# Second mixture-of-experts layer: token rows turned a step or two later for two tiles, check counts issued later, gathers issued one part per step

## The chip, the cores and the metric

The kernel runs on one core of a Trainium2 chip. The metric is the time of one execution on the device in microseconds (us). Before the change the median of three runs is 853.89 us (852.45 to 854.54).

Engines are named as the profile names them: PE is TensorE (its matmuls; PEld are its weight loads), DVE is VectorE, ACT is ScalarE, POOL is GpSimd, SP is SyncE. Each engine works through its own instructions in order. SBUF is the on-chip memory; PSUM is the small memory into which PE writes, in banks.

## The reference

Three layers follow each other. Only the last one is touched by the change.

```python
def reference(**kwargs):
    attn_out = _attn_ref(**attn_kwargs)                 # 4 x 8 heads, 768 positions, window 128 and 4 sink keys
    x = np.ascontiguousarray(attn_out.transpose(0, 2, 1, 3)).reshape(B * S, H * D)   # 3072 tokens x 512
    x = _moe_ref(x=x, **moe_kwargs)                     # 8 experts, the best one per token, scaled by its gate
    return _moe2_ref(x=x, **moe2_kwargs)

def _moe2_ref(x, w_gate, w1, w2):
    N, D = x.shape                                      # 3072, 512
    E = w_gate.shape[1]                                 # 8 experts
    cap = N // E                                        # each takes 384 tokens
    logits = x @ w_gate
    order = np.argsort(-logits.flatten())
    assigned, counts = -np.ones(N, int), np.zeros(E, int)
    for idx in order:                                   # best (token, expert) pairs first
        tok, e = idx // E, idx % E
        if assigned[tok] >= 0 or counts[e] >= cap:
            continue
        assigned[tok] = e; counts[e] += 1
    for e in range(E):
        mask = assigned == e
        out[mask] = np.maximum(x[mask] @ w1[e], 0) @ w2[e]
    return out
```

## The kernel before

The last layer (function `moe2`) handles eight **tiles**, numbered 0 to 7 here. A tile is one expert with its 384 tokens. Which expert fills up first, and with which tokens, is not known until the chip has worked it out, so the routing of tile k+1 runs on the side while PE multiplies tile k.

**The multiplication** (`Ffn.run`). A tile has 8 steps, one for each block of 128 hidden values. In step s PE makes 12 matmuls of the first layer (`ph`, line 1036), ACT and DVE split the result into two parts (`hh`, `hl`, lines 1046 and 1047), and PE makes 9 matmuls of the second layer for the block of two steps earlier (`y`, line 950). Every number is carried as a high and a low part, so three matmuls stand for one. The inner function `side(q)` is called at four places of a step, q = 0 to 3: after half of the first layer, after the rest of it, after the first three matmuls of the second layer, and at its end. There a weight block is split (ACT makes `w1h` and `w2h`, DVE or POOL makes `w1l` and `w2l`), the rows of the next tile are turned, and the routing goes a piece on (`tick`).

**Rows of the next tile.** POOL gathers the 384 token rows of a tile by three indirect DMAs of 128 rows (`xget`, line 1893), then copies the expert's number (`em3`), for which the load of the second half of the weights waits. The rows are **turned** in four parts, d = 0 to 3: three transpositions by PE into the PSUM bank `tr` (line 796), then ACT copies them out (`xh`, line 797) and DVE makes the rest (`xl`, line 798). The bank `tr` exists once, so a turn waits until ACT and DVE have emptied it of the turn before. The table `xp=((6, 0), (6, 2), (7, 0), (7, 2))` says where: part 0 in step 6 at q = 0, part 1 in step 6 at q = 2, and so on.

**The routing** (`Route.steps`, `compact_steps`). Tokens of an expert are found by a search for a threshold: DVE compares (`cmp`), PE counts (`rt<-OH,cmp`, line 1693), DVE reduces, PE spreads the result (line 1976), DVE sets the next bound, two to four times per tile. Then comes the **compaction**: sums on PE (line 1498), ranks on DVE (`r`), one-hot rows in two halves and their factors on DVE (`ohb`, `ft`), and a chain of 26 matmuls on PE (`rc<-ft,ohb`, line 1523), from which DVE reads the row numbers (`idx`). Two **check counts** stand beside it: the number of tokens taken (`rc<-A,ones`, line 1517, read by ACT at line 1902 into `ckj`) and the number of tokens by expert (`rc<-OH,ones`, lines 1967 and 2033, read by ACT into `ckm`). They are only compared with what they should be at the very end. All of these write to different columns of one PSUM tile, `rc`. POOL copies one number per search step (`hold`, line 1957), between its other work.

The order on each engine is the order in which the code issues it. The generators of the routing are advanced at every `tick`; they go on when a small model of the clock, kept while the program is built, says that PE and DVE are far enough.

Of the kernel before, what the change touches and what calls it, by code (L numbers as in the profile page):

```python
# [13 lines left out]
I32 = mybir.dt.int32  # L14
# [11 lines left out]
E, F = 8, 1024  # L26
# [753 lines left out]
class Ffn:  # L780
# [37 lines left out]
    def warm(self, k):  # L818
        p = self.ps.tile([128, 512], F32, name="y0")
        for _ in range(k):  # L820
            self.nc.tensor.matmul(p, self.g.wz[:, 0:128], self.g.wz, start=True, stop=True)

    def run(self, js, w1, w2, src, yout, hook=None, xp=((6, 0), (6, 2), (7, 0), (7, 2)), LEAD=3, LAG=2, pre=None, onx=None, more=(), mark=lambda s, n: None):


        nc, wk, ps, clk = self.nc, self.wk, self.ps, self.g.clk
# [47 lines left out]
        def poll_x():  # L874
            if wantx and (wantx[0] == js[0] or st[0] >= min(8 * alljs.index(wantx[0]) - XO, total - 8)) and src.ready_x(wantx[0]):
                j = wantx[0]
                if j not in asked:
                    src.xids(j)
                    asked[j] = src.wait
                if asked[j] == 0:  # L880
                    xgs[wantx.pop(0)] = src.xget(j)
                else:
                    asked[j] -= 1
# [48 lines left out]
        def prep(j, d, tag="tr"):  # L932
            if j not in xgs:
                src.force_x(j)
                clk.pe = max(clk.pe, clk.dve)
                wantx.remove(j)
                xgs[j] = src.xget(j)
            if d == 0 and onx is not None:
                onx(j, xgs[j])
            self.xprep(j, src.width(j), xgs[j], d, tag)  # L940

        def tick():
            if hook is not None:
                hook()
            poll_w(2)
            poll_x()

        def mm3(o, pairs, w, first, end):
            for i, (l, r) in enumerate(pairs):
# [41 lines left out]
        for s in range(last + 1):  # L991
            st[0] = s
            jx, f = divmod(s, 8)

            def side(q):
                while q == 3 and late:
                    split(*late.pop(0))
                ticked = q == 3 and not self.vsplit and s + LEAD < total and (s + LEAD) % 2 == 0 and not late
                if ticked:
                    tick()  # L1000
                if q == 1 and late:
                    late.append((s, 1))
                else:
                    split(s, q)
                if jx + 1 < len(js) and s < total:
                    for d in range(4):
                        if xp[d] == (f, q):
                            prep(js[jx + 1], d)
                if not ticked:
                    tick()  # L1010

            if s < total and small(s):
                q = f % 4
# [39 lines left out]
            if s in second:  # L1053
                c = second[s][0]
                j1, f1 = divmod(c, 8)
                A = src.width(js[j1])
# [4 lines left out]
                parts = [(hh, hl, w2h, w2l, f1)]  # L1061
# [37 lines left out]
class Src:  # L1099
# [13 lines left out]

    force_x = xids = force_e
    wait = 0

    def ereg2(self, j):
        return self.ereg(j)
# [348 lines left out]
JC, NIT, FEW, IDLE = 64, 4, 2, (3, 2, 1)  # L1467
# [9 lines left out]
WT = 3, 2, (3, 6), (1, 3), 6, 2, 3, 9, 2, 2  # L1477
# [4 lines left out]
def compact_steps(nc, g, p, pi, A, rs, pre, tag, check=None, warm=lambda k: None, tcol=None, lag=0.2, wt=0, first=None):  # L1482

    clk = g.clk
    V = Vec(nc, clk)
    iob, tcol = g.iob, tcol or g.tcol
    n = A.shape[1]
    H = half(n)
    nd = tcol.shape[2]
    k = nd // 2  # L1490
    bs, acc, cnt = pi[:, 0:1], pi[:, 32:32 + 3 * nd], pi[:, 64:64 + n]
    pj = p.tile([128, k, 4], F32, name=tag + "pj", bufs=1)
    r = p.tile([128, 4, n], F32, name=tag + "r", bufs=1) if first is None else first
    r0, g0, g1, g2 = (r[:, i] for i in range(4))
    rb = p.tile([128, n], BF, name=tag + "rb", bufs=1)
    oh = p.tile([128, 2, 128, H], BF, name=tag + "ohb", bufs=1)
    ft = p.tile([128, n, nd, 3], BF, name=tag + "ft", bufs=1)
    nc.tensor.matmul(bs, g.tri, rs, start=True, stop=True, skip_group_check=True)
    nc.scalar.activation(g0, A, AF.Copy)
    warm(wt)  # L1500
    yield 0.0
    V.scalar_tensor_tensor(r0, pre, bs, A, op0=OP.add, op1=OP.mult)
    V.tensor_scalar(g1, r0, 128.5, None, op0=OP.is_ge)
    V.tensor_scalar(g2, r0, 256.5, None, op0=OP.is_ge)
    V.scalar_tensor_tensor(r0, g1, -128.0, r0, op0=OP.mult, op1=OP.add)
    V.scalar_tensor_tensor(rb, g2, -128.0, r0, op0=OP.mult, op1=OP.add)
    yield 0.0
    cuts = [(0, 0, H)] + ([(1, 0, n - H)] if first is None else [(1, 0, 8), (1, 8, n - H)])
    for q, o, w in cuts:
        V.tensor_tensor(oh[:, q, :, o:w], iob[:, :, 0:w - o], bc(rb[:, None, H * q + o:H * q + w], [128, 128, w - o]), op=OP.is_equal)  # L1510
        if q == 0:
            V.tensor_tensor(ft, bc(r[:, 1:4, :, None].rearrange("p a n w -> p n w a"), [128, n, nd, 3]),
                            bc(tcol[:, 0:n, :, None], [128, n, nd, 3]), op=OP.mult)
        yield 0.0
    V.memset(pj[:, :, 3:4], 0.0)
    if check is not None:
        nc.tensor.matmul(cnt, g.ones, A, start=True, stop=True, skip_group_check=True)
        check(cnt)
    warm(WT[4])
    yield clk.dve + lag  # L1520
    tiles = [t for t in range(n) if n != NR or t % HR <= HT]
    for t in tiles:
        nc.tensor.matmul(acc, oh[:, t // H, :, t % H], ft[:, t], start=(t == 0), stop=(t == tiles[-1]),  # L1523
                         skip_group_check=True)
    clk.mm(64 * n)
    V.tensor_reduce(pj[:, :, 0:3], acc.rearrange("p (k w a) -> p k a w", w=2, a=3), axis=AX.X, op=OP.add)
    out = []
    for i, top in enumerate((NSL, N) if k == 2 else (N,)):
        out.append(p.tile([128, 3], I32, name=f"{tag}idx{i}", bufs=E))
        V.scalar_tensor_tensor(out[i], pj[:, i, 1:4], float(top), pj[:, i, 0:3], op0=OP.add, op1=OP.subtract)  # L1530
    return out
# [19 lines left out]
class Route(Src):  # L1551
# [337 lines left out]

    def xget(self, k):  # L1890
        xg = self.x[k] if k in self.x else self.xp.tile([128, 3, DM], F32, name="xg2", bufs=2)
        for a in range(3):
            self.nc.gpsimd.indirect_dma_start(out=xg[:, a, :], out_offset=None, in_=self.xs,
                                              in_offset=bass.IndirectOffsetOnAxis(ap=self.idx[k][0][:, a:a + 1], axis=0))
        em = self.em3[k] = self.p.tile([1, 1], I32, name="em3", bufs=E)
        self.nc.gpsimd.tensor_copy(em, self.e[k])
        return xg

    def compact(self, k, A, rs, pre):
        def check(cnt):  # L1900
# [13 lines left out]
    def steps(self):  # L1914
        nc, g, p = self.nc, self.g, self.p
        clk = g.clk
# [14 lines left out]
        for k in range(E):  # L1931
            A = p.tile([128, NR], BF, name="A", bufs=E)
# [94 lines left out]
            else:  # L2027
# [2 lines left out]
                V.tensor_scalar(t0, esum, -1.0, float(E * (E - 1) // 2), op0=OP.mult, op1=OP.add)  # L2030
                V.tensor_scalar(t0, t0, 0.0, float(E - 1), op0=OP.max, op1=OP.min)
                V.tensor_copy(em, t0[0:1])
                nc.tensor.matmul(pc, g.ones, OH, start=True, stop=True, skip_group_check=True)
                nc.scalar.activation(junk, pc, AF.Copy, accum_out=chk[:, 0, k:k + 1])
                self.e[k] = em
                self.comp.append(self.compact(k, A, rs, pre))
                yield 0.0


def moe2(tc, g, rt, w1, w2, out):  # L2040
    nc = tc.nc
    with ExitStack() as ctx:
        ctx.enter_context(tc.manual_schedule())
        f = Ffn(ctx, tc, g, "m2")
        rt.ps, rt.xp, rt.warm = f.ps, f.wk, f.warm
        rt.prime()

        puts = []
        spacer = f.wk.tile([1, 1], F32, name="spacer", bufs=1)

        def yout(k, a, y):
            yr = f.wk.tile([128, DM], F32, name="yr", bufs=4)
            nc.scalar.activation(yr, y, AF.Copy)
            nc.gpsimd.memset(spacer, 0.0)
            st = nc.gpsimd.indirect_dma_start(out=out, out_offset=bass.IndirectOffsetOnAxis(
                ap=rt.idx[k][1][:, a:a + 1], axis=0), in_=yr, in_offset=None, bounds_check=N - 1, oob_is_err=False)
            for o in puts:
                tc.declare_no_dep(st.ins, o.ins, reason="rows of other tokens")
            puts.append(st)
            if k < E - 1 and a == 2:  # L2060
                nc.gpsimd.drain()

        f.run(list(range(E)), w1, w2, rt, yout, hook=rt.pop, xp=((6, 0), (6, 2), (7, 0), (7, 2)))
        bi = g.cp.tile([1, 1], I32, name="bi")
        nc.vector.tensor_copy(bi, rt.bad[0:1])
    return nc.values_load(bi, min_val=0, max_val=1)
# [214 lines left out]
```

## Time and profile before

| | before |
|---|---|
| median of 3 runs | 853.89 us |
| profiled execution, whole | 853.57 us |
| its span in the trace | 851.8 us |
| PE busy (matmuls) | 813.5 us, 96% of the span |
| DVE busy | 608.7 us, 71% |
| ACT busy | 384.9 us, 45% |
| POOL busy | 348.0 us, 41% |
| eight tiles of the last layer | from about 524 to 846 us of the span |

The span is what the trace covers from the first to the last instruction; the profiled execution took 1.8 us more than its span. Times in rows of the trace are microseconds from the start of the span. PE's matmuls are pipelined: of two matmuls in a row the second starts about 0.17 us after the first, though each is shown with a length of 0.34 us. So the cost of a stretch on PE is read from start to start.

### The profile page before, as it was taken

What the parts mean: (1) busy time and instruction counts of PE and PEld (TensorE: products, weight loads), DVE (VectorE), ACT (ScalarE), POOL (GpSimd) and SP (SyncE); (2) the same over time, 40 slices, a digit from 0 to 9 for tenths busy, and PEclk for the clock granted to TensorE, in tenths of its full rate; (3) what the DMA queues carried; (4) which work ended last, traced back from release to release, by engine and by line L of the source; (5) the groups of instructions that cost most, each with busy time, mean ns of one, the idle gap of its engine ahead of it and who ended that gap; (6) DMA issues with size and microseconds to landing.
All of it is one profiled execution on the core that took longest, in us unless ns stands there. A gap on an engine that the chain in (4) does not pass through costs nothing.

```text
span 851.8 us, 15197 instructions
## 1 busy us (share of the span) xinstructions
PE 813.5 (96%) x5001; PEld 651.6 (76%) x5006; DVE 608.7 (71%) x1763; ACT 384.9 (45%) x1091; POOL 348.0 (41%) x574
## 2 busy tenths in 40 slices
PE   8889999998999999999999988999999999999997
PEld 4666666667888888888888746778888888889996
DVE  7888787877579696978878268868688787753320
ACT  6667777764342433344342313334334343434442
POOL 5455967582331101020000004436465656465662
PEclk9999999999999999999999998999999999999999
DMA  7434555666534544444436507334444345345401
GB/s 222 159 107 150 151 144 143 176 217 215 120 84 166 161 136 149 149 148 126 124 104 223 192 14 235 126 110 149 145 155 146 129 151 154 126 161 174 147 39 42
DMA packets 70655, 122.85 MB, mean 144 GB/s; under 512 B 9890, under 2 KB 24102, under 8 KB 70440
## 3 DMA queue, kind: packets, MB, share of 16 engines
q1 hardware_dynamic: 63848, 102.36, 38.0%
q0 software_dynamic: 6720, 19.43, 7.1%
q8 instruction: 42, 0.69, 0.4%
q14 instruction: 45, 0.37, 0.2%
HBM read 102.06 MB, written 19.71 MB: 143 GB/s over the span
## 4 chain that ended last, share of the span: by engine, by line
PE 78%; DVE 11%; ACT 4%; issue 3%; DMA 1%; POOL 1%; DVEq 0%; POOLq 0%; ACTq 0%
PE y L950 29%; PE ph L1036 28%; PE sp L323 4%; PE po L395 3%; ACT P L352 3%; PE tr L796 2%; PE rt L1693 2%; PE pt L360 2%; PE px L431 1%; PE rc L1523 1%; DMA xg<-xs,idx 1%; DVE mx L342 1%; DVE sc L145 1%; PE sp L409 1%; DVE sp L340 1%
## 5 line engine op out<-in xcount | busy, mean ns | idle before, releaser
L1046 ACT ACTIVATE hh<-ph 128x384 fp32r<-128x384 f32 (+1 forms) x112 | 60.2, 538 | 268.2 <-PE ph L1036 267.6
L1036 PE MATMUL ph<-xh,w1h 128*128 128x384 f32 (+1 forms) x448 | 166.9, 372 | 0.8 <-DVE hl L1047 0.8
L1036 PE MATMUL ph<-xh,w1l 128*128 128x384 f32 (+1 forms) x448 | 161.1, 360 | 1.2 <-DVE w1l L922 1.2
L1036 PE MATMUL ph<-xl,w1h 128*128 128x384 f32 (+1 forms) x448 | 160.4, 360 | 0.0
L950 PE MATMUL y<-w2h,hh 128*128 128x512 f32 x384 | 153.6, 400 | 0.0
L950 PE MATMUL y<-w2h,hl 128*128 128x512 f32 x384 | 150.9, 393 | 0.0
L950 PE MATMUL y<-w2l,hh 128*128 128x512 f32 x384 | 150.5, 392 | 0.0
L1047 DVE SCALAR_TENSOR_TENSOR hl<-ph,hh 128x384 fp32r<-128x384 f32 (+1 forms) x112 | 68.4, 612 | 98.6 <-ACT hh L1046 98.1
L1201 POOL DMA_INDIRECT xg<-xd,ent x26 | 28.0, 1078 | 195.0 <-DMA ent<-idtab 189.8
L1225 DVE SCALAR_TENSOR_TENSOR junk<-yr,wgb 128x512 f32<-128x512 f32 x160 | 103.1, 685 | 0.0
L901 POOL TENSOR_TENSOR w2l<-w2r,w2h 128x512 fp32r<-128x512 f32 x60 | 79.2, 1326 | 46.1 <-ACT w2h L897 22.2
L1036 PEld LDWEIGHTS ph<-xh,w1h 128*128 128x128 f32 x448 | 85.0, 190 | 12.6 <-issue 1.9
L1036 PEld LDWEIGHTS ph<-xh,w1l 128*128 128x128 f32 x448 | 84.3, 188 | 11.1 <-DVE w1l L922 1.6
L352 ACT ACTIVATE P<-sp,mx 128x132 f32<-128x132 f32 x192 | 69.3, 369 | 51.5 <-DVE mx L342 18.7
L1036 PEld LDWEIGHTS ph<-xl,w1h 128*128 128x128 f32 x448 | 84.0, 188 | 7.7
L950 PEld LDWEIGHTS y<-w2h,hl 128*128 128x128 f32 x384 | 72.0, 188 | 15.6
L950 PEld LDWEIGHTS y<-w2h,hh 128*128 128x128 f32 x384 | 72.6, 189 | 11.5 <-issue 0.2
L950 PEld LDWEIGHTS y<-w2l,hh 128*128 128x128 f32 x384 | 72.2, 188 | 11.7
L323 PE MATMUL sp<-kr,qs 64*128 64x260 f32 (+1 forms) x384 | 58.6, 402 | 13.7 <-ACT P L352 12.5
L917 ACT ACTIVATE w1h<-w1r 128x512 fp32r<-128x512 f32 x108 | 67.3, 624 | 2.1 <-DVE lp L449 2.1
L897 ACT ACTIVATE w2h<-w2r 128x512 fp32r<-128x512 f32 x108 | 67.5, 625 | 0.0
L922 DVE TENSOR_TENSOR w1l<-w1r,w1h 128x512 fp32r<-128x512 f32 x78 | 63.8, 818 | 2.4 <-ACT w1h L917 2.4
(394 smaller groups left out, 1401.9 us busy)
## 6 DMA issues: line engine op xcount, KB each, us to landing
w1r<-in_w_dram SPq DMA_DIRECT2D x29, 1024.0 KB, 5.8
w2r<-in_w_dram SPq DMA_DIRECT2D x29, 1024.0 KB, 5.9
vr<-in_v_dram SPq DMA_DIRECT2D x16, 384.0 KB, 4.9
xd<-xb SPq DMA_DIRECT2D x16, 384.0 KB, 3.5
xs<-yr SPq DMA_DIRECT2D x24, 256.0 KB, 6.1
kr<-in_kT_dram SPq DMA_DIRECT2D x15, 396.0 KB, 3.8
qr<-in_qT_dram SPq DMA_DIRECT2D x15, 384.0 KB, 4.3
wgb<-in_wg2T_dram SPq DMA_DIRECT2D x1, 2048.0 KB, 8.4
```

The source lines that it names most:

```text
L323: nc.tensor.matmul(sp[:, hd, c0:260], qs[o:o + 64, 128 * i:128 * i + 128], kr[o:o + 64, k0:k0 + 260 - c0], start=True, stop=True)
L352: nc.scalar.activation(z.P[:, n % 2, hd, :], s.sp[:, hd, 128:260], AF.Exp, bias=s.mx[:, hd:hd + 1], accum_out=z.sm[:, n % 2, hd:hd + 1])
L897: nc.scalar.activation(ch[1][c][0], r[q // 2][:, q % 2, :] if isinstance(r, list) else r[:, q, :], AF.Copy)
L901: eng.tensor_tensor(lo, r[q // 2][:, q % 2, :] if isinstance(r, list) else r[:, q, :], h.bitcast(F32), op=OP.subtract)
L917: nc.scalar.activation(h, v, AF.Copy)
L922: eng.tensor_tensor(lo, v, h.bitcast(F32), op=OP.subtract)
L950: nc.tensor.matmul(o, l, r, start=(first and i == 0), stop=(end and i == 2))
L1036: nc.tensor.matmul(ph, wp[:, c, :], xp_[:, c, 0:NTK], start=(d == 0 and i == 0), stop=(d == 3 and i == len(cut[d]) - 1))
L1046: nc.scalar.activation(hh, ph, AF.Relu)
L1047: nc.vector.scalar_tensor_tensor(hl, ph, 0.0, hh.bitcast(F32), op0=OP.max, op1=OP.subtract)
L1201: self.nc.gpsimd.indirect_dma_start(out=self.xg[j][:, a, :], out_offset=None, in_=self.G.xd[0:k, :], in_offset=bass.IndirectOffsetOnAxis(a ...
L1225: nc.vector.scalar_tensor_tensor(junk, yr[:, 0:DM], 1.0, wgb[:, e, :], op0=OP.mult, op1=OP.mult, accum_out=lg[:, e:e + 1])
```

## The change

Four edits, all in the last layer. `run` gets a second table `xp2`, used for the turns of tiles 1 and 2. The token count of a compaction is issued after the wait for the one-hot rows instead of before it. The count by expert of the last tile is issued a piece of the routing later. And the three gathers of tiles 3 to 7 (`k > FEW`, FEW is 2) are issued one per `tick`.

```diff
@@ Ffn.run @@
-    def run(self, js, ..., mark=lambda s, n: None):
+    def run(self, js, ..., mark=lambda s, n: None, xp2=None):
...
                 xgs[j] = src.xget(j)
+            src.more()
...
             poll_w(2)
-            poll_x()
+            if src.parts:
+                src.more(1)
+            else:
+                poll_x()
...
                     for d in range(4):
-                        if xp[d] == (f, q):
+                        if (xp2 if xp2 and jx < 2 else xp)[d] == (f, q):
                             prep(js[jx + 1], d)
@@ compact_steps @@
     V.memset(pj[:, :, 3:4], 0.0)
+    warm(WT[4])
+    yield clk.dve + lag
     if check is not None:
         nc.tensor.matmul(cnt, g.ones, A, start=True, stop=True, skip_group_check=True)
         check(cnt)
-    warm(WT[4])
-    yield clk.dve + lag
@@ Route @@
     def xget(self, k):
         xg = self.x[k] if k in self.x else self.xp.tile([128, 3, DM], F32, name="xg2", bufs=2)
-        for a in range(3):
+
+        def part(a):
             self.nc.gpsimd.indirect_dma_start(out=xg[:, a, :], out_offset=None, in_=self.xs,
                                               in_offset=bass.IndirectOffsetOnAxis(ap=self.idx[k][0][:, a:a + 1], axis=0))
-        em = self.em3[k] = self.p.tile([1, 1], I32, name="em3", bufs=E)
-        self.nc.gpsimd.tensor_copy(em, self.e[k])
+            if a == 2:
+                em = self.em3[k] = self.p.tile([1, 1], I32, name="em3", bufs=E)
+                self.nc.gpsimd.tensor_copy(em, self.e[k])
+        self.parts = [lambda a=a: part(a) for a in range(3)]
+        self.more(1 if k > FEW else 3)
         return xg
+
+    def more(self, n=3):
+        for f in self.parts[0:n]:
+            f()
+        del self.parts[0:n]
@@ Route.steps, last tile @@
-                nc.tensor.matmul(pc, g.ones, OH, start=True, stop=True, skip_group_check=True)
-                nc.scalar.activation(junk, pc, AF.Copy, accum_out=chk[:, 0, k:k + 1])
                 self.e[k] = em
                 self.comp.append(self.compact(k, A, rs, pre))
+                yield max(clk.dve, clk.pe) + 1.0
+                nc.tensor.matmul(pc, g.ones, OH, start=True, stop=True, skip_group_check=True)
+                nc.scalar.activation(junk, pc, AF.Copy, accum_out=chk[:, 0, k:k + 1])
                 yield 0.0
@@ moe2 @@
-        f.run(list(range(E)), w1, w2, rt, yout, hook=rt.pop, xp=((6, 0), (6, 2), (7, 0), (7, 2)))
+        f.run(list(range(E)), w1, w2, rt, yout, hook=rt.pop, xp=((6, 0), (6, 2), (7, 0), (7, 2)), xp2=((6, 2), (7, 0), (7, 1), (7, 2)))
```

What this does to the order on the engines is shown at three places. Line numbers of the changed kernel are 4 to 18 higher (1036 becomes 1040, 950 becomes 954, 1523 becomes 1531).

PE, steps 6 and 7 of tile 0, in which the rows of tile 1 are turned; `tr` is the bank into which they are turned, `xg` holds the gathered rows. Before, part 0 at q = 0 and part 1 at q = 2 of step 6:

```order
L1036 MATMUL ph<-xl,w1h 128x384
L796 MATMUL tr<-cst,xg_6934 128x128 x3
L1036 MATMUL ph<-xh,w1h 128x384
L1036 MATMUL ph<-xh,w1l 128x384
L1036 MATMUL ph<-xl,w1h 128x384
L1036 MATMUL ph<-xh,w1h 128x384
L1036 MATMUL ph<-xh,w1l 128x384
L1036 MATMUL ph<-xl,w1h 128x384
L950 MATMUL y_6741<-w2h,hh 128x512
L950 MATMUL y_6741<-w2l,hh 128x512
L950 MATMUL y_6741<-w2h,hl 128x512
L796 MATMUL tr<-cst,xg_6934 128x128 x3
```

Of the changed kernel, step 7, where its parts 1, 2 and 3 now stand (parts 2 and 3 are in this piece):

```order
L1040 MATMUL ph<-xl,w1h 128x384
L796 MATMUL tr<-cst,xg_6934 128x128 x3
L954 MATMUL y_6741<-w2h,hh 128x512
L954 MATMUL y_6741<-w2l,hh 128x512
L954 MATMUL y_6741<-w2h,hl 128x512
L796 MATMUL tr<-cst,xg_6934 128x128 x3
```

Part 0 moved behind six matmuls of the first layer and three of the second; part 1 to step 7, q = 0; part 2 from there to q = 1, so that only three matmuls of the second layer stand between it and part 3.

PE, the compaction of tile 4; `rc` is the PSUM tile that both counts and the chain write, and "waits" names the engine whose semaphore an instruction waits for. Before, at the chain's begin:

```order
L950 MATMUL y_8418<-w2h,hh 128x512
L950 MATMUL y_8418<-w2l,hh 128x512 [waits Pool_49]
L950 MATMUL y_8418<-w2h,hl 128x512
L1523 LDWEIGHTS ohb [waits DVE_49]
L1523 MATMUL rc<-ft,ohb 128x12 [waits Activation_49]
```

And now:

```order
L954 MATMUL y_8415<-w2h,hl 128x512
L1527 LDWEIGHTS ones
L1527 MATMUL rc<-A,ones 128x28 [waits Activation_49]
L1531 LDWEIGHTS ohb [waits DVE_49]
L1531 MATMUL rc<-ft,ohb 128x12 [waits Activation_49]
```

The token count, which stood 38 rows ahead of the chain, before a search count, now stands right in front of the chain. The chain's first matmul waits for ACT in both; the wait's value is that of ACT's reading of the last count before it, which was `ckm` here and is `ckj` of this very token count now. All eight compactions have this order now.

POOL, the gathers of tile 4; `xg` is what they fill, `w1l` and `w2l` are weight blocks that POOL splits. Before:

```order
L901 TENSOR_TENSOR w2l<-w2r,w2h 128x512
L1893 DMA xg_8458<-xs,idx_8454 128x512 x3
L1896 COPY em_8462<-em 1x1
L1957 COPY hold<-sc 1x1
L922 TENSOR_TENSOR w1l<-w1r,w1h 128x512
L901 TENSOR_TENSOR w2l<-w2r,w2h 128x512
```

And now:

```order
L901 TENSOR_TENSOR w2l<-w2r,w2h 128x512
L1902 DMA xg_8458<-xs,idx_8454 128x512
L1974 COPY hold<-sc 1x1
L922 TENSOR_TENSOR w1l<-w1r,w1h 128x512
L1902 DMA xg_8458<-xs,idx_8454 128x512 x2
L1906 COPY em_8488<-em 1x1
L901 TENSOR_TENSOR w2l<-w2r,w2h 128x512
```

The copy `hold` and one weight block moved ahead of the second and third gather. SP's queue keeps its order.

## Rows read from the trace of the kernel before

**Rows 1.** Waits of PE, 520 to 825 us: us in total, times, longest
```profile
PE tr L796 <- DMA xg<-xs,idx: 3.2, 4, 1.1
PE rt L1693 <- DVE cmp L145: 1.1, 1, 1.1
PE rc L2033 <- DVE OH L145: 0.7, 1, 0.7
PE rc L1517 <- DVE r L145: 0.6, 1, 0.6
```

**Rows 2.** Timeline, turn of tile 1: start, length, engine, line, operation [idle before]
```profile
552.45 0.34 PE L1036 MATMUL ph<-xl,w1h 128*128 128x384 f32 x1
...
555.25 0.33 PE L796 MATMUL tr<-cst,xg 128*128 128x128 f32 x1 [1.13 <-DMA xg<-xs,idx]
...
555.34 0.42 PE L1036 MATMUL ph<-xh,w1h 128*128 128x384 f32 x1
```

**Rows 3.** Timeline, first turn of tile 2, and a turn without a wait
```profile
597.98 0.34 PE L1036 MATMUL ph<-xl,w1h 128*128 128x384 f32 x1
...
600.04 0.42 PE L1036 MATMUL ph<-xh,w1h 128*128 128x384 f32 x1
...
604.61 0.34 PE L1036 MATMUL ph<-xl,w1h 128*128 128x384 f32 x1
...
605.03 0.42 PE L1036 MATMUL ph<-xh,w1h 128*128 128x384 f32 x1
```

**Rows 4.** Chain that ended last, from part 0 to part 1
```profile
555.58 1.04 PE ph L1036 x6
556.62 0.69 PE y L950 x3
```

**Rows 5.** Timeline, how long the bank is held: tile 1, then tile 2
```profile
560.98 0.49 PE L796 MATMUL tr<-cst,xg 128*128 128x128 f32 x3
...
561.36 1.09 DVE L145 TENSOR_TENSOR cmp<-ub,iou 128x1792 bf16<-128x1792 bf16 x1
...
562.74 0.55 DVE L798 TENSOR_TENSOR xl<-tr,xh 128x384 fp32r<-128x384 f32 x1
...
563.35 0.55 PE L796 MATMUL tr<-cst,xg 128*128 128x128 f32 x3
...
604.78 0.49 PE L796 MATMUL tr<-cst,xg 128*128 128x128 f32 x3
...
605.31 0.49 ACT L797 ACTIVATE xh<-tr 128x384 fp32r<-128x384 f32 x1 [1.88 <-PE tr L796]
...
605.84 0.56 DVE L798 TENSOR_TENSOR xl<-tr,xh 128x384 fp32r<-128x384 f32 x1 [0.41 <-ACT xh L797]
```

**Rows 6.** Timeline, a token count and ACT's reading of it, compaction of tile 7
```profile
754.14 0.19 PE L1517 MATMUL rc<-A,ones 128*128 128x28 bf16 x1
...
754.43 0.19 ACT L1902 ACTIVATE ckj<-rc 128x28 f32<-128x28 f32 x1 [1.71 <-PE rc L1517]
754.52 0.19 ACT L1902 ACTIVATION_READ_ACCUMULATOR ckj<-rc 128x1 f32 x1
```

**Rows 7.** Timeline, ACT at the chain of tile 4's compaction
```profile
662.78 0.62 ACT L917 ACTIVATE w1h<-w1r 128x512 fp32r<-128x512 f32 x1
...
662.90 1.73 PE L1523 MATMUL rc<-ft,ohb 128*128 128x12 bf16 x26
```

**Rows 8.** Timeline, second half of the one-hot rows, compaction of tile 1
```profile
545.88 1.08 DVE L145 TENSOR_TENSOR ohb<-iob,rb 128x1792 bf16<-128x1792 bf16 x1
```

**Rows 9.** Timeline, DVE beside POOL: tile 3's gathers, then tile 4's
```profile
631.62 0.96 POOL L1893 DMA_INDIRECT xg<-xs,idx  x1 [0.31 <-issue]
631.74 0.35 DVE L145 SCALAR_TENSOR_TENSOR sc<-J8m,dd,sc 128x1 f32<-128x1 f32 x2
...
672.11 3.18 DVE L145 SCALAR_TENSOR_TENSOR sc<-J8m,dd,sc 128x1 f32<-128x1 f32 x2
...
673.86 1.28 POOL L901 TENSOR_TENSOR w2l<-w2r,w2h 128x512 fp32r<-128x512 f32 x1
```

More of the change, by code (lines that the diff above doesn't have):

```diff
@@ L821, in warm, with run @@
             self.nc.tensor.matmul(p, self.g.wz[:, 0:128], self.g.wz, start=True, stop=True)
-    def run(self, js, w1, w2, src, yout, hook=None, xp=((6, 0), (6, 2), (7, 0), (7, 2)), LEAD=3, LAG=2, pre=None, onx=None, more=(), mark=lambda s, n: None):
+    def run(self, js, w1, w2, src, yout, hook=None, xp=((6, 0), (6, 2), (7, 0), (7, 2)), LEAD=3, LAG=2, pre=None, onx=None, more=(), mark=lambda s, n: None, xp2=None):
         nc, wk, ps, clk = self.nc, self.wk, self.ps, self.g.clk
@@ L1115 @@
     wait = 0
+    parts = ()
+    def more(self, n=3):
+        pass
     def ereg2(self, j):
@@ L1891, in xget, with more @@
         xg = self.x[k] if k in self.x else self.xp.tile([128, 3, DM], F32, name="xg2", bufs=2)
-        for a in range(3):
+        def part(a):
             self.nc.gpsimd.indirect_dma_start(out=xg[:, a, :], out_offset=None, in_=self.xs,
                                               in_offset=bass.IndirectOffsetOnAxis(ap=self.idx[k][0][:, a:a + 1], axis=0))
-        em = self.em3[k] = self.p.tile([1, 1], I32, name="em3", bufs=E)
-        self.nc.gpsimd.tensor_copy(em, self.e[k])
-        return xg
+            if a == 2:
[3 more added lines that the diff above has]
+        self.more(1 if k > FEW else 3)
+        return xg
+    def more(self, n=3):
+        for f in self.parts[0:n]:
+            f()
+        del self.parts[0:n]
     def compact(self, k, A, rs, pre):
@@ L2032, in steps @@
                 V.tensor_copy(em, t0[0:1])
+                self.e[k] = em
+                self.comp.append(self.compact(k, A, rs, pre))
+                yield max(clk.dve, clk.pe) + 1.0
                 nc.tensor.matmul(pc, g.ones, OH, start=True, stop=True, skip_group_check=True)
                 nc.scalar.activation(junk, pc, AF.Copy, accum_out=chk[:, 0, k:k + 1])
-                self.e[k] = em
-                self.comp.append(self.compact(k, A, rs, pre))
                 yield 0.0
```

## The prediction

> **What bounds the kernel now.** I read the page first: PE is busy for 96% of the span, the next engine, DVE, for 71%. Then I asked for the waits of PE alone in the last layer. There the reader is to see how little there is to win: the search for rows that have not landed (3.2 us in four waits), one wait for a comparison (1.1), one for the one-hot of the last tile's count (0.7), one for the ranks `r` (0.6) [rows 1]. PE runs on without a gap otherwise, so what is taken from it or put on it moves the end by the same amount, unless a later wait swallows it. The timeline then says what each wait costs, and the order of instructions where the edits put new ones. I use the profiled execution, 853.57 us, and add 0.32 at the end, by which it lies under the median of 853.89.
>
> **Turns of tiles 1 and 2: what goes.** In tile 1, part 0 costs PE 555.34 - 552.45 = 2.89 us from the matmul before to the matmul after [rows 2]; the same turn without a wait costs 605.03 - 604.61 = 0.42 [rows 3]. So 2.47 us are lost to the third gather, which lands at 555.25. In tile 2 it is 600.04 - 597.98 - 0.42 = 1.64 [rows 3]. Now part 0 stands behind six matmuls of the first layer and three of the second, 1.04 + 0.69 = 1.73 us [rows 4]. In tile 1 PE arrives at 552.45 + 0.17 + 1.73 = 554.35, turns two thirds in 0.22 and waits from 554.57 until 555.25: 0.68 are left. In tile 2 it arrives 1.73 after 598.15, which is just when the rows are there (600.04 less the last transposition); nothing is left.
>
> **What comes for it.** The four parts now stand closer, and `tr` is one bank. From the start of a turn the bank is held until DVE ends `xl`: 605.84 + 0.56 - 604.78 = 1.62, and PE starts the next turn 0.06 later (`xl` ends at 563.29, the turn starts at 563.35) [rows 5]: 1.68 us. Between parts 1 and 2 there are now a turn and six matmuls, 0.33 + 1.06 = 1.39: 0.29 short. Between parts 2 and 3 a turn and three matmuls, 0.33 + 0.69 = 1.02: 0.66 short. That is 0.95 in each tile. In tile 1 it is worse: part 1 now stands where part 2 stood, at 560.98 in rows of before, and its `xl` is queued on DVE behind the comparison that runs from 561.36 for 1.09 us; the bank is free for a turn at 563.35, while PE wants it at 560.98 + 1.39 = 562.37: 0.98 instead of 0.29. Before, the same comparison cost PE 0.55 - 0.33 = 0.22 at that turn [rows 5], which goes. Tile 1: -2.47 + 0.68 + 0.98 + 0.66 - 0.22 = -0.37. Tile 2: -1.64 + 0.95 = -0.69. Together **-1.06 us**. Bounds: -4.11 if the bank never makes PE wait and the rows are there; +1.2 if each of the four new bank waits is longer by the 0.55 of an `hl` or `xl` ahead of it in the queue.
>
> **Token counts.** This is the term that I take for the largest. The count now stands directly in front of the chain of 26 matmuls, and the chain's first matmul waits until ACT has read the count. A wait of that kind is there in the trace: before, the count in the compaction of tile 1 waited 0.6 us for DVE's `r`, which reads another column of `rc` [rows 1]. Columns don't matter; the tile does. What it costs: the count starts at 754.14, ACT begins to read at 754.43 and its second part ends at 754.52 + 0.19 = 754.71 [rows 6]. That is 0.57 from the count's start, and 0.63 with the 0.06 in which PE picks up; the chain would have started some 0.08 after the count anyway. So 0.55 us of PE standing still, where it had worked. In the compactions of tiles 4 and 5 ACT is not free: its `w1h` ends at 662.78 + 0.62 = 663.40, while the chain began at 662.90 [rows 7], so reading starts 0.18 later than 0.29 after the count; two tiles, 0.36. Tiles 2 to 7 are six chains: 6 x 0.55 + 0.36 = **+3.66 us**. Tiles 0 and 1 cost nothing, since there the chain waits for the second half of the one-hot rows anyway: in tile 1 DVE ends it at 545.88 + 1.08 = 546.96 [rows 8], and the wait for ACT is over before. For the same reason the 0.6 us that PE no longer waits for `r` there is not won: PE only comes earlier to the same one-hot rows. Bounds for the six: 0 if PE has no wait after all, 6 x 1.2 = 7.2 if ACT is each time still busy with `hh` and `w1h`, twice some 0.6 [rows 7].
>
> The Trainium skill, "PSUM — Partial Sum Buffer", section "PSUM bank collisions raise a hardware error", says that accesses of two engines are to be kept apart by bank and 32-partition quadrant, not by address. The 0.6 us wait for `r` agrees. By that rule the counts cost their 3.66 us; if addresses were what counts, the sum below would be 851.1.
>
> **Count by expert of the last tile.** Its wait of 0.7 us for the one-hot [rows 1] goes: the count now comes when that has long been made, and the 0.26 us of matmul are the same: **-0.7 us**. What is late next there is nothing that the rows show; the range is 0 to -0.7.
>
> **Gathers one by one.** They decide nothing by landing later, as far as I see: a third part starts later by a `w1l` or `w2l` (1.28 [rows 9]) or two and a `hold`, and the turns of tiles 3 to 7 waited for no rows before; the four waits in rows of before are those of tiles 1 and 2 [rows 1]. What they change is what POOL does beside DVE. In tile 4, DVE's two operations on 128 single numbers take 3.18 us, from 672.11 to 675.29, until just after POOL's `w2l` ends (673.86 + 1.28 = 675.14); during a gather the same two took 0.35 (631.74, inside 631.62 to 632.58) [rows 9]. The late comparison is PE's 1.1 us wait [rows 1]. Now `w1l` stands ahead of the second and third gather, so that POOL is gathering when DVE comes to these operations: **-1.1 us**. Bounds: -1.1, and +1.1 if instead another search step of tiles 3 to 7 falls beside POOL's `w1l` and `w2l`. I take the end that the order gives for this place.
>
> The Trainium skill, "SBUF — State Buffer", section "SBUF: two separate sides", says that GpSimd and a DVE operation with two SBUF inputs exclude each other for a whole instruction when the GpSimd operation reads SBUF. The 3.18 against 0.35 agrees. By it the gain at tile 4 is had, and each shift of POOL's splits can make a new such stop; without it the sum would be 855.9.
>
> **Sum.** -1.06 + 3.66 - 0.7 - 1.1 = +0.8 us, 853.57 + 0.8 = 854.4 for the profiled execution, and with 0.32 for a median **854.7 us**: the waits taken from PE come back as waits on ACT. A measurement of this kernel can't tell less than about 0.3% (2.6 us) from no change, so faster is under 851.3 and slower over 856.5.
>
> **Rivals.**
> *The chain doesn't stand still.* If PE has other work or ACT's reading is covered in the six chains, 854.7 - 3.66 = 851.1. For it: before, the chain had a wait on ACT too and none shows in its rows. Against: there, the reading had ended long before; now nothing stands between count and chain. 0.20.
> *ACT is busy at every chain.* ACT works in order, and `hh` and `w1h` of the step stand ahead of the reading. If at all six chains PE comes to the count before `hh` has begun, each wait grows by about 0.6 (1.2 instead of 0.6): 854.7 + 6 x 0.6 = 858.3. For it: in tile 4 `w1h` is still running when the chain begins [rows 7]. Against: there it costs only 0.18, since several matmuls of the second layer lie between. It decides from 0.5 us more per chain. 0.15.
> *Turns win nothing.* If part 0 still waits as long, since the third gather lands later beside other transfers, or if the third part of tile 3's rows, now behind `hold` and a `w2l` of 1.28 us, lands after its turn: 854.7 + 1.06 = 855.8. 0.15.
> The forecast has 0.50.
>
> **How the numbers follow.** Of the forecast's 0.50, with terms that may miss by 2 us together, 0.05 lie under 851.3, 0.08 over 856.5. The first rival sits at the bound: 0.13 faster, 0.07 the same. The second: 0.12 slower, 0.03 the same. The third: 0.12 the same, 0.03 slower. Faster 0.18, same 0.59, slower 0.23. The range of 8 in 10 runs from 850.9, a little under the first rival, to 857.8, most of the way to the second.
>
> **What would show each step.** In the waits of PE: the line for the gathers falls from 3.2 to about 0.7, a line turn for `xl` rises to some 2 to 3 us, a line of the chain for `ckj` appears with 6 waits of about 0.55, the lines for the last count and for `r` go. The comparison's 1.1 us goes, and the 3.18 in tile 4 becomes about 0.35. It would be wrong if PE's chain starts right behind the count; if the turns' waits for `xl` stay under 0.3 us; or if PE waits for a comparison in other tiles than 4.

## The result: 861.4 us, 1% slower, and the profile after

The changed kernel took 861.37 us (median of 6 runs, 860.26 to 864.75) beside 853.37 for the kernel before (6 runs on the same chip): a ratio of 1.0099, 95% interval 1.0078 to 1.0119. The forecast was 854.7, and its range ended at 857.8. The profiled execution took 860.60 us, span 858.9, with a mean granted TensorE clock of 0.981; the one of before had 853.57, 851.8 and 0.992. That last pair holds the answer.

First the view with which the prediction began, PE's waits in the last layer of the changed kernel (us in total, times, longest):

```profile
PE rc L1531 <- ACT ckj L1919: 2.6, 6, 0.5
PE tr L796 <- DVE xl L798: 1.8, 3, 0.8
PE ph L1040 <- DVE hl L1051: 0.8, 1, 0.8
PE tr L809 <- DMA xg<-xs,idx: 0.6, 1, 0.6
PE tr L796 <- DMA xg<-xs,idx: 0.6, 1, 0.6
PE rc L1531 <- DVE ft L145: 0.5, 1, 0.5
PE rc L1506 <- DVE A L145: 0.4, 1, 0.4
```

Beside [rows 1] nearly all is as forecast: the gathers' 3.2 us in four waits are one of 0.6, a line for `xl` and a line of six waits for `ckj` have come, the comparison, `OH` and `r` are gone. By this view the kernel is not slower: its lines add up to 7.3 us, and the same view of before to 7.4 (the waits of 0.8, 0.6 and 0.4 us for `hl`, for `xg` at line 809 and for `A` stand in both). None of the prediction's three signs of being wrong has come; all three were about waits. So the question is where along the program the 7 us arise. The chains of 26 small matmuls stand at known places in both kernels. The timeline of before, chains of tiles 2, 3 and 7 (that of tile 4 is in [rows 7]) and the last matmul of all:

```profile
588.65 1.73 PE L1523 MATMUL rc<-ft,ohb 128*128 128x12 bf16 x26
626.99 1.73 PE L1523 MATMUL rc<-ft,ohb 128*128 128x12 bf16 x26
756.70 1.73 PE L1523 MATMUL rc<-ft,ohb 128*128 128x12 bf16 x26
845.21 0.39 PE L950 MATMUL y<-w2h,hl 128*128 128x512 f32 x1
```

and of after, chains of tiles 2, 3, 4 and 7, and the last matmul:

```profile
588.94 1.67 PE L1531 MATMUL rc<-ft,ohb 128*128 128x12 bf16 x26 [0.38 <-ACT ckj L1919]
629.90 1.67 PE L1531 MATMUL rc<-ft,ohb 128*128 128x12 bf16 x26 [0.38 <-ACT ckj L1919]
669.23 1.67 PE L1531 MATMUL rc<-ft,ohb 128*128 128x12 bf16 x26 [0.54 <-ACT ckj L1919]
762.70 1.67 PE L1531 MATMUL rc<-ft,ohb 128*128 128x12 bf16 x26 [0.43 <-ACT ckj L1919]
852.71 0.39 PE L954 MATMUL y<-w2h,hl 128*128 128x512 f32 x1
```

The changed kernel is late by 0.29 us at tile 2's chain, 2.91 at tile 3's, 6.33 at tile 4's, 6.00 at tile 7's and 7.50 at the end. Three steps of 2.6, 3.4 and 1.5 us, behind the chains of tiles 2, 3 and 7, are nearly all of it; between the chains of tiles 4 and 7 it makes up 0.33. The windows view behind the chains of tiles 2, 3, 4 and 7 shows what the first, second and fourth of these places have in common (stretch, length, PE busy and in brackets its matmuls, granted clock, DMA share, GB/s). After:

```profile
592.20:599.00 6.80, 6.80 (x23) 0.57 0.60 147
633.20:640.00 6.80, 6.80 (x22) 0.57 0.62 205
671.00:674.40 3.40, 3.40 (x19) 1.00 0.00 0
765.30:768.80 3.50, 3.50 (x13) 0.51 1.05 393
```

and before, behind the same chains:

```profile
592.00:598.80 6.80, 6.62 (x43) 1.00 0.51 154
630.40:637.20 6.80, 6.80 (x46) 1.00 0.78 270
664.60:668.00 3.40, 3.40 (x20) 1.00 0.01 5
760.10:763.50 3.40, 3.40 (x19) 1.00 1.03 380
```

PE never stands still there, and yet in the first two stretches it does about half as many matmuls (23 and 22 for 43 and 46) and in the last 13 for 19: the granted clock has fallen to its lower level, 1.2 GHz, for most of these three. The third, behind tile 4's chain, keeps the full clock. The chain that ended last shows it in the durations (start, us, what):

```profile
588.94 1.67 PE rc L1531 x26
590.62 0.82 PE y L954 x3
591.43 0.77 PE rt L1701 x13
592.21 2.12 PE ph L1040 x6
594.36 2.13 PE ph L1040 x6
596.49 2.86 PE y L954 x9
```

Six matmuls of the first layer take 2.12 us, where before they took 1.04 [rows 4]. With PE at work throughout, a stretch loses its length times what is missing from the clock: 6.8 x 0.43 = 2.92 at tile 2 and as much at tile 3, 3.5 x 0.49 = 1.72 at tile 7, and 3.3 us with 0.86 and 0.85 directly ahead of the first two, 0.46 and 0.50: together 8.5 us. With what the waits cost and the edits win, that makes the 7 us. Ahead of each fall PE waited some 0.4 us for `ckj`, then did 26 matmuls of 12 columns. But the chains of tiles 4, 5 and 6 have the same wait and no fall.

### The profile page after: what moved, and what is told of

Its sections match the earlier page's. It is cut to its first block, busy times and chain, and to the rows that moved or that the text cites. A ratio compares the mean times of both kernels' runs of the same rounds, so it can differ in the third digit from the quotient of the medians.

```text
span 858.9 us, 15216 instructions
## 1 busy us (share of the span) xinstructions
PE 822.5 (96%) x5006; PEld 659.1 (77%) x5006; DVE 604.7 (70%) x1763; ACT 384.4 (45%) x1091; POOL 347.8 (40%) x574
## 4 chain that ended last, share of the span: by engine, by line
PE 78%; DVE 10%; ACT 5%; issue 4%; POOL 1%; DMA 1%; DVEq 0%; POOLq 0%; ACTq 0%
PE ph L1040 28%; PE y L954 28%; PE sp L323 4%; PE po L395 3%; ACT P L352 3%; PE tr L796 2%; PE rt L1701 2%; PE pt L360 2%; PE px L431 1%; PE rc L1531 1%; DVE mx L342 1%; PE sp L409 1%; DMA xg<-xs,idx 1%; DVE sp L340 1%; PE ph L1316 1%
## 5 line engine op out<-in xcount | busy, mean ns | idle before, releaser
L1040 PE MATMUL ph<-xh,w1h 128*128 128x384 f32 (+1 forms) x448 | 169.2, 378 | 0.8 <-DVE hl L1051 0.8
L1040 PE MATMUL ph<-xh,w1l 128*128 128x384 f32 (+1 forms) x448 | 163.3, 365 | 1.2 <-DVE w1l L922 1.2
L1040 PE MATMUL ph<-xl,w1h 128*128 128x384 f32 (+1 forms) x448 | 162.8, 366 | 0.0
L922 DVE TENSOR_TENSOR w1l<-w1r,w1h 128x512 fp32r<-128x512 f32 x78 | 61.1, 783 | 2.4 <-ACT w1h L917 2.4
```

Of the source, the lines that this page charges most:

```text
L922: eng.tensor_tensor(lo, v, h.bitcast(F32), op=OP.subtract)
L1040: nc.tensor.matmul(ph, wp[:, c, :], xp_[:, c, 0:NTK], start=(d == 0 and i == 0), stop=(d == 3 and i == len(cut[d]) - 1))
```

## The experiments

Theory A: the wait directly ahead of the small matmuls is what lets the clock fall, and the price is the clock, not the wait. Rivals: the falls come from another part of the change; or a row of small matmuls, or a wait, is enough by itself. Every ratio is to the kernel before on the same chip; the clock is the mean granted clock over a kernel's timed runs. The kernel before has 0.991 or 0.992 there. The rows come from several chips, so times of different rows are best compared by their ratios.

| kernel | us | ratio, 95% interval | clock |
|---|---|---|---|
| changed | 861.37 | 1.0099 [1.0078, 1.0119] | 0.980 |
| changed, a second time | 861.42 | 1.0105 [1.0086, 1.0124] | 0.980 |
| count at its old place | 852.53 | 0.9985 [0.9966, 1.0003] | 0.991 |
| before + count alone | 860.91 | 1.0082 [1.0055, 1.0108] | 0.983 |
| count behind the chain | 851.28 | 0.9971 [0.9953, 0.9989] | 0.991 |
| wait filled, 3 matmuls | 854.14 | 1.0007 [0.9989, 1.0026] | 0.992 |
| wait filled, 1 matmul | 855.77 | 1.0028 [1.0006, 1.0050] | 0.990 |
| count copied twice | 861.42 | 1.0119 [1.0103, 1.0135] | 0.983 |
| count copied four times | 867.01 | 1.0172 [1.0149, 1.0195] | 0.980 |
| wait elsewhere, 1 copy | 855.58 | 1.0037 [1.0023, 1.0051] | 0.990 |
| wait elsewhere, 2 copies | 856.77 | 1.0050 [1.0029, 1.0070] | 0.990 |
| wait at the chain, 1 copy | 856.54 | 1.0039 [1.0022, 1.0056] | 0.987 |
| wait at the chain, 2 copies | 860.70 | 1.0089 [1.0068, 1.0109] | 0.985 |
| before + turns alone | 852.47 | 0.9990 [0.9975, 1.0005] | 0.991 |
| before + gathers alone | 851.35 | 0.9978 [0.9967, 0.9990] | 0.991 |
| before + last count alone | 853.65 | 1.0012 [0.9994, 1.0030] | 0.991 |
| before + count behind alone | 853.15 | 1.0006 [0.9994, 1.0018] | 0.990 |
| count behind, old turns | 851.81 | 0.9991 [0.9978, 1.0004] | 0.991 |
| count behind, tile 1's turns | 852.21 | 1.0006 [0.9991, 1.0021] | 0.989 |

**Is it the token count?** The count back at its old place in the changed kernel, and the count alone moved in the kernel before:

```diff
-    warm(WT[4])
-    yield clk.dve + lag
     if check is not None:
         nc.tensor.matmul(cnt, g.ones, A, start=True, stop=True, skip_group_check=True)
         check(cnt)
+    warm(WT[4])
+    yield clk.dve + lag
```

(the first; the second is the same edit the other way round, in the kernel before).

> The changed kernel with the token count of every compaction issued where it stood before the change (ahead of the yield, not directly ahead of the chain of 26 matmuls); turns, split gathers and the late last count as in the change. Theory A (TensorE's wait for ScalarE's copy of the count, directly ahead of the chain, is what lets the granted clock fall to half in three stretches; price of the falls about 8.5 us, of the waits themselves 2.6 to 3.7): both go, no half-clock stretch after 540 us, 861 - 8.5 - 3 = about 850 us. Theory B (the falls come from another part of the change, or from a shift in time): only the waits go, falls stay, about 858 us. Theory C (no fall matters, the time is lost elsewhere): 860 or more.

> The kernel before with this one part of the change: the token count issued directly ahead of the chain. Theory A: six waits of about 0.5 us and two or three half-clock stretches behind a chain of 26 small matmuls, 853.4 + 3 + 5 to 9 = 861 to 865 us. Theory B: the six waits alone, 853.4 + 3 = 856 to 857 us, full clock after tile 0. Theory C: as before, 853.4 within 1 us.

The clock comes back to 0.991 and the time to 852.5 in the one, they go to 0.983 and 860.9 in the other. That is theory A's clock in both, and its time to within 0.1 us in the second; in the first its 850 was 2.5 us too low. The rivals in which another part of the change makes the falls, or no fall matters, are out. The waits themselves are no explanation; PE's waits for `ckj` in the second kernel:

```profile
PE rc L1523 <- ACT ckj L1902: 2.7, 6, 0.5
```

2.7 us, and `r` and the comparison no longer among its waits, against 8 us of time.

**Is it the standing still?** Two ways to take the wait away and keep the work: the count behind the chain, and three matmuls on zeros in the place of the wait.

```diff
-    if check is not None:
-        nc.tensor.matmul(cnt, g.ones, A, start=True, stop=True, skip_group_check=True)
-        check(cnt)
     tiles = [t for t in range(n) if n != NR or t % HR <= HT]
     for t in tiles:
         nc.tensor.matmul(acc, oh[:, t // H, :, t % H], ft[:, t], ...)
+    if check is not None:
+        nc.tensor.matmul(cnt, g.ones, A, start=True, stop=True, skip_group_check=True)
+        check(cnt)
```

```diff
         check(cnt)
+        if cover is not None:      # tiles 2 to 7
+            cover(3)               # 3 matmuls wz[:, 0:128] x wz into bank tr
```

> The changed kernel with the token count behind the chain of 26 matmuls instead of ahead of it; the count and its copy are still done, but no matmul of the chain waits for the copy. Theory A: no wait inside the chain, full clock after 540 us, about 850 us (850 to 852). Theory B: falls stay, 858 us.

> The changed kernel with three more matmuls of 512 columns on zeros (into the free bank of the turns) between the token count and the chain, in the compactions of tiles 2 to 7: TensorE has work where it waited for the copy. They cost about what the wait cost (3 x 0.22 us against 0.5). Theory A: the chain's wait shrinks to 0.1 us or less, the clock stays full, time falls by the price of the falls alone: 861 - 8.5 + 1 = about 853.5 us. Theory B: falls stay, about 861 to 862 us.

851.28 and 854.14, clock 0.991 and 0.992. The second is the plainest: more work than in the changed kernel, and 7 us less. Its timeline at tile 2:

```profile
588.19 0.19 PE L1532 MATMUL rc<-A,ones 128*128 128x28 bf16 x1
588.23 0.81 PE L826 MATMUL tr<-wz 128*128 128x512 bf16 x3
588.87 1.67 PE L1538 MATMUL rc<-ft,ohb 128*128 128x12 bf16 x26
...
592.43 0.34 PE L1045 MATMUL ph<-xl,w1h 128*128 128x384 f32 x1
```

The chain follows without a gap, and the matmuls behind it have their 0.34 us of the full clock. The count behind the chain beats the changed kernel, and the kernel before by 0.1 to 0.5%.

**A wait alone, or only at the small matmuls?** On the kernel with the count behind the chain, a wait of PE for ACT was added in tiles 2 to 7, once some steps earlier among wide matmuls, once directly ahead of the chain; each with one copy by ACT, and with two (`for _ in range(2)` around the copy).

```diff
+    def stall(self):
+        p = self.ps.tile([128, 512], F32, name="tr", bufs=self.trbufs)
+        j = self.wk.tile([128, NR], F32, name="stj")
+        mm = lambda: self.nc.tensor.matmul(p[:, 0:NR], self.g.wz[:, 0:128], self.g.wz[:, 0:NR], start=True, stop=True)
+        mm()
+        self.nc.scalar.activation(j, p[:, 0:NR], AF.Copy)
+        mm()
```

> The changed kernel with the token count behind the chain (851.3 us, clock 0.991), plus, in tiles 2 to 7, a wait of TensorE for ScalarE among wide matmuls: a matmul of 28 columns on zeros into the bank of the turns, ScalarE's copy of it, and a second such matmul that has to wait for the copy, issued some steps ahead of the chain. Theory A with both needed (wait and row of small matmuls): the six waits alone, 851.3 + 6 x 0.5 to 0.7 = 854.5 to 855.5 us, clock 0.990. Rival (a wait of that length is enough anywhere): falls as in the changed kernel, 861 or more, clock 0.980.

> The same as the run before, but with the wait on the turns' bank directly ahead of the chain of 26 matmuls. No matmul of the chain waits for the count; PE stands still just ahead of the chain for another reason. Theory A: falls come back, 860 to 864 us, clock 0.978 to 0.984. Rival (it is the count's own place or its bank, not the standing still): 854.5 to 855.5 us, clock 0.990, as among wide matmuls.

> The kernel with the added wait among wide matmuls, with the copy done twice as well. If only the place beside the row of small matmuls matters: 855.6 + 6 x 0.2 = 856.8 us, clock 0.989 to 0.991. If a wait of this length is enough anywhere: 860 to 862 us, clock below 0.984.

> The kernel with the added wait on the turns' bank directly ahead of the chain, with ScalarE's copy in it done twice, so that each wait is some 0.5 us instead of 0.3. If the length up to 0.4 us decides: 856.5 + 6 x 0.2 + 2 to 4 = 860 to 862 us, clock 0.979 to 0.983, as in the changed kernel. If the place of the count decides (its matmul and copy ahead of the chain): 857.5 to 858.5 us, clock 0.986 to 0.988.

Among wide matmuls the waits brought 855.6 and 856.8 with a clock of 0.990. By the ratios that is 5.6 and 6.7 us over the kernel without them, for waits of 2.3 and 3.6 us in the profiles: some 3 us beyond their length, which the runs explain only in part (a clock of 0.990 instead of 0.991 is about 1 us), and which a second copy does not raise. At the chain the short wait missed what A said (856.5, 0.987); the longer one met it, 860.7, with 0.985 where 0.979 to 0.983 was expected. The waits in the two kernels with two copies, elsewhere and at the chain, are alike in length:

```profile
PE tr L826 <- ACT stj L829: 3.6, 6, 1.1
```

```profile
PE tr L826 <- ACT stj L829: 3.4, 6, 0.7
```

and 3.9 us lie between their times, measured on one chip. So the place decides, at an equal wait: it is the wait directly ahead of the small matmuls that is dear. The length matters too. At tile 2's chain, one copy and two:

```profile
592.05 0.17 PE L826 MATMUL tr<-wz 128*128 128x28 bf16 x1 [0.28 <-ACT stj L828]
```

```profile
589.17 0.17 PE L826 MATMUL tr<-wz 128*128 128x28 bf16 x1 [0.51 <-ACT stj L829]
```

The profiles of all runs can be counted, chains of tiles 2 to 7 and the stretch right behind each. With a wait of 0.38 us or more directly ahead, 19 of 38 chains lost the clock; with a wait of 0.21 to 0.32 us (one copy at the chain, one filler), none of 7; in the ten kernels with no such wait, none of 60. With the wait elsewhere two of 12 did, both tile 3's, 8.8 us behind the wait; so a fall there is rare but not excluded. Two things are not shown. What it is in this row of matmuls (12 columns each, every one with its own weight load) that counts was not varied. And the added waits with two copies, 0.57 us on average, left the clock at 0.985, where the changed kernel's 0.43 us left 0.980, so the length is not all.

**Does a longer wait make more falls?** One filler instead of three in the changed kernel (`cover(1)`); ACT's copy of the count done twice, and four times (`for _ in range(4 if k > 1 else 1)` around it); and the changed kernel again beside them.

> The changed kernel with one matmul of 512 columns on zeros between the token count and the chain (tiles 2 to 7) instead of three: about 0.2 of the 0.5 us of each wait is filled, so 0.3 us stay. Theory A in its graded form (the shorter the wait, the fewer falls): mean granted clock between that of the changed kernel (0.980) and that with three (0.992), 855 to 859 us. Theory A in an all-or-nothing form: 0.992 and about 853 us, or 0.980 and about 861.

> The changed kernel with ScalarE's copy of the token count done twice in tiles 2 to 7, so that each of the six waits ahead of the chain grows from 0.5 to about 0.8 us. Theory A: more half-clock stretches than the three of the changed kernel, 861.4 + 6 x 0.3 + 3 to 9 = 866 to 872 us, mean granted clock below 0.975. Rival (what counts is the row of small matmuls, not the wait): only the waits grow, 861.4 + 1.7 = about 863 us, clock 0.980.

> The changed kernel itself once more, beside the next three on one chip: 861.4 us (860 to 865), mean granted clock 0.980, as a measure for them. Theory A needs both above 859 us and below 0.985; if it is nearer 854 here, the price of the falls differs from chip to chip.

> The changed kernel with ScalarE's copy of the token count done four times in tiles 2 to 7: waits of some 1.1 to 1.3 us instead of 0.45, 6 x 0.75 = 4.5 us more of waiting. Graded form of theory A (more standing still, more falls): 861.4 + 4.5 + 2 to 6 = 868 to 872 us, clock 0.970 to 0.977. All-or-nothing form (a wait of 0.4 us already brings all the falls that the place allows): 866 us, clock 0.980.

One filler leaves waits of up to 0.3 us and clock 0.990. Its 855.8 us lie in the range of the graded form, the clock near the full end; from the run with three fillers the intervals don't tell it apart. The waits for `ckj` of the kernels with two copies and with four:

```profile
PE rc L1531 <- ACT ckj L1920: 4.5, 6, 0.9
```

```profile
PE rc L1531 <- ACT ckj L1920: 8.4, 6, 1.5
```

Two copies missed both expectations: 1.9 us more of waiting and no more time, with a clock of 0.983 instead of 0.980. By the clock alone that gives back some 2.6 us (an estimate: 0.003 of 861), about what the waits add. Four copies came out as the all-or-nothing form says, 5.6 us more than the changed kernel and the same 0.980. So from some 0.4 us on a longer wait costs at most its length and brings no further falls.

**Which of the six chains?** In the second profile of the changed kernel, the stretches behind the chains of tiles 2, 3, 4, 6 and 7:

```profile
591.50:598.20 6.70, 6.70 (x26) 0.56 0.64 172
632.00:638.80 6.80, 6.80 (x52) 1.00 0.69 217
669.90:673.30 3.40, 3.40 (x14) 0.62 0.26 77
...
751.80:755.20 3.40, 3.40 (x12) 0.62 0.00 0
765.40:768.80 3.40, 3.40 (x14) 0.61 1.00 301
```

Not the same ones: tile 3's chain kept the clock, those of tiles 4 and 6 lost it. The same kernel pays in other places from run to run, and its time is nearly the same. The places are not evenly spread, though: in the six profiles with waits of 0.38 us or more at all six chains, tile 2's lost the clock five times and tile 5's never, though the wait at tile 5 was among the longest each time (0.54 us in the changed kernel).

**The other parts, each alone in the kernel before, and what is left of the turns.** The edits are the parts of the change itself; "count behind alone" is the diff shown above without the rest, "old turns" drops `xp2`, "tile 1's turns" uses it for `jx < 1`.

> The kernel before with this one part: rows of the second and third tile turned one or two steps later. By the prediction's term: gather waits of 2.5 and 1.6 us go, waits for the lower parts of the bank copies (xl) of 0.98 + 0.66 + 0.95 come, sum -1.06: about 851.6 to 852 us beside 852.7. Rival (the gathers are waited for somewhere else, nothing gained): 852.7 to 853. Clock full after tile 0 by both.

> The kernel before with this one part: gathers of tiles beyond the third issued one part per step. By the prediction's term: the wait of 1.1 us for the comparison beside a gather's issue goes, about 851.6 us beside 852.7. Rival (the wait moves to the next step whose vector work falls on GpSimd's work): 852.7 within 0.5.

> The kernel before with this one part: the count by expert of the last tile issued 1 us later. By the prediction's term: the wait of 0.7 us for OH goes, about 852.0 us beside 852.7. Rival: the wait turns into one of a matmul of the compaction for the count's copy (1.1 us stood there with the token count at its old place), 852.7 to 853.1.

> The kernel before with the token count behind the chain of 26 matmuls and nothing else changed. Theory A (what counts is whether a matmul waits for the copy): 852.7 within 0.5, the wait for r of 0.6 us may go (852.1), clock full after tile 0. Rival (small matmuls in a row lower the clock by themselves, the wait is not needed): one or more half-clock stretches and 856 or more.

> The changed kernel with the token count behind the chain and with the turns of the second and third tile back at their old steps (the gathers split, the last count late). What the turns are worth beside the other parts: by the prediction's term 1.06 us, by the run of that part alone 0.4 us. Expected 851.7 to 852.4 beside 851.3 for the same kernel with the later turns; if the later turns cost something here, below 851.3. Clock full after tile 0.

> The changed kernel with the token count behind the chain and only the second tile's rows turned later; the third tile's at the old steps. By the prediction's terms the third tile's later turns are worth 1.64 - 0.95 = 0.7 us, so about 852.0; if its bank waits cost as much as its gather wait, 851.3 as with both.

The gathers win by themselves, 0.9 to 2.8 us by the interval. The turns alone can't be told from nothing. Beside the count behind the chain they can't either: 0.9991 with the old turns, 0.9971 with the later ones, and the intervals overlap. The late last count wins nothing alone, as its rival said: in that kernel its matmul waits for the token count's copy instead.

```profile
742.75 0.26 PE L2036 MATMUL rc<-OH,ones 128*128 128x224 bf16 x1 [1.14 <-ACT ckj L1902]
```

The count behind the chain alone changes nothing that can be measured (853.15). With only tile 1's rows turned later a comparison is waited for again; its waits have this line:

```profile
PE rt L1701 <- DVE cmp L145: 1.8, 1, 1.8
```

## Why the prediction was wrong, step by step

*Turns, -1.06:* the right mechanism, a little more gain. The rows of after that answer to [rows 2, 3, 5], one turn each, three of tile 1 and one of tile 2:

```profile
555.22 0.33 PE L796 MATMUL tr<-cst,xg 128*128 128x128 f32 x1 [0.61 <-DMA xg<-xs,idx]
...
561.36 0.55 PE L796 MATMUL tr<-cst,xg 128*128 128x128 f32 x3 [0.81 <-DVE xl L798]
...
563.08 0.55 PE L796 MATMUL tr<-cst,xg 128*128 128x128 f32 x3 [0.48 <-DVE xl L798]
...
609.17 0.55 PE L796 MATMUL tr<-cst,xg 128*128 128x128 f32 x3 [0.47 <-DVE xl L798]
```

0.61, 0.81 and 0.48 stand for the forecast's 0.68, 0.98 and 0.66 in tile 1, 0.47 for 0.95 in tile 2: -0.79 and -1.17, together -1.96. The fourth bank wait of the forecast, 0.29 between parts 1 and 2 of tile 2, did not come. The part alone measured 0.9990, or -0.9 us (-2.1 to +0.4).

*Token counts, +3.66:* the failed step. The waits came, as rows 6 and 7 had said, 2.6 us in all: 0.38 to 0.43 at four chains where the forecast had 0.55, and 0.54 at tiles 4 and 5 where it had 0.73. ACT at tile 4's chain:

```profile
668.38 0.62 ACT L917 ACTIVATE w1h<-w1r 128x512 fp32r<-128x512 f32 x1
668.91 0.18 ACT L1919 ACTIVATE ckj<-rc 128x28 f32<-128x28 f32 x1
```

It comes to `ckj` behind `w1h`, which made that wait 0.54; the rival in which ACT is busy at every chain did not happen. What failed is the price: "0.55 us of PE standing still" was taken as the whole cost, with every other matmul at its length of before. By the runs the count alone costs 0.82% (0.55 to 1.08), 4.7 to 9.2 us, of which at most 2.7 are waits. The rest is the granted clock: 8.5 us in the profile of after. No rival had it; the second's 858.3 lies nearest to the measured time, but by another mechanism, which did not happen. The profile of before gave no such case in the last layer's chains, since no wait stood directly ahead of a chain of tiles 2 to 7 there, though its page shows the clock as a row of its own.

*Last count, -0.7:* its wait is gone in the changed kernel. It is won only because the token count was moved too.

*Gathers, -1.1:* right in sign and place, not quite in the reason; alone -1.9 (-2.8 to -0.9). The 3.18 us of [rows 9] did not fall to 0.35; DVE's two operations in tile 4 after, and POOL's split beside them:

```profile
678.42 1.81 DVE L145 SCALAR_TENSOR_TENSOR sc<-J8m,dd,sc 128x1 f32<-128x1 f32 x2
...
678.80 1.28 POOL L901 TENSOR_TENSOR w2l<-w2r,w2h 128x512 fp32r<-128x512 f32 x1
```

The forecast had POOL gathering when DVE comes to them. Its last gather ended at 678.65, 0.23 us after DVE began, and DVE again ended just after a split. But before, two splits stood there in a row (`w1l` from 672.61, `w2l` from 673.86), and now one does. 1.81 us were short enough that PE no longer waited for the comparison.

*Sum:* the terms as measured in rows are -1.96 + 2.6 - 0.7 - 1.1 = -1.2, so 853.57 - 1.2 = 852.4 with the clock as before, and 860.9 with its 8.5; the profiled execution took 860.60. Side sums of the prediction are off by up to 0.1 us (851.0 without the counts, 855.8 without the gathers); nothing hangs on that.

The Trainium skill, "TensorE: Matmul & The Clock Gate", section "A second HAM failure mode: psum-queue depth-cycling", tells of a kernel in which frequent small idle times between groups of matmuls sent the clock back and forth between its two levels. The runs here agree that short waits can go with falls (0.38 to 0.54 us, clock 0.980). They add that one such wait per tile cost far less of the clock among wide matmuls than ahead of the small ones (0.990 against 0.985).

Open is whether it is more than chance that two copies left a higher clock than one, what decides which of the six chains loses the clock, and what in the row of small matmuls counts.

## What to carry to other kernels

In this kernel a wait of PE had two prices: its length, and the clock of what followed when it stood directly ahead of a row of small matmuls. Before an edit puts a matmul whose result another engine must read into the same PSUM tile just ahead of such a row, put it behind the row (0.9971 here), or put wide work in between (1.0007). When waits add up and the time doesn't, compare the granted clock of both kernels stretch by stretch before anything else.

## What the runs showed of the hardware

A stretch at the lower clock looks fully busy: PE busy 6.80 of 6.80 us, clock 0.57. It is seen in the clock column and in the lengths of equal matmuls (0.52 for 0.34 us), not in the waits or the busy share.

The clock fell in other places too. In the kernel with only the count behind the chain, tile 2's turn, matmuls of 128 columns with a wait between them, came ahead of one:

```profile
599.16 0.33 PE L796 MATMUL tr<-cst,xg 128*128 128x128 f32 x1 [1.11 <-DMA xg<-xs,idx]
...
599.89 0.52 PE L1036 MATMUL ph<-xh,w1h 128*128 128x384 f32 x1
```

In the kernel before, the timed runs go from 851.19 us at a mean clock of 0.996 to 859.78 at 0.981: much of what looks like the noise of this kernel goes with the clock.
